# A fused attention and GLU kernel: results stored without the doubled rest, block 0's rest copied at once, stored sums added a step later

## The chip, the cores and the metric

The kernel runs on one core of a Trainium2 chip. The core's engines each work through a queue of their own: TensorE (PE in the profile, with its weight loads as PEld) multiplies matrices, VectorE (DVE) and ScalarE (ACT) do elementwise work, GpSimd (POOL) here does little besides issuing stores, and SyncE (SP) issues loads. An engine takes its instructions strictly in order, so an instruction that waits holds everything behind it on that engine. The metric is the device time of the whole program in microseconds; lower is better.

## The reference

Input `x` has 2048 tokens of 576 features. There are 32 heads of 18, and each token attends to 8 earlier tokens at a distance of 2 (itself included). What is computed, cut to what matters:

```python
def _A_ref(x, wqkv, wo):                      # attention
    qkv = (x @ wqkv).reshape(B, S, 3, 32, 18) ...
    idx = pos[:, None] - (arange(8) * 2)[None, :]
    logits = einsum("bhsd,bhswd->bhsw", q, kg) * scale   # masked where idx < 0
    o = einsum("bhsw,bhswd->bhsd", softmax(logits), vg)
    return o.reshape(B, S, 576) @ wo
def _B_ref(x, w_gate, w_up, w_down):          # GLU, hidden width 4608
    return (sigmoid(x @ w_gate) * (x @ w_up)) @ w_down
h  = x + _A_ref(_layernorm(x), wqkv, wo)
h2 = h + _B_ref(_layernorm(h), w_gate, w_up, w_down)
```

## The kernel before

**Blocks.** The 2048 tokens are cut into four blocks of 512 (even and odd tokens, first and second half), each held as four tiles of 128 tokens. Heads come in four groups `g` of 8 heads (144 columns). An attention unit (b, g) is the attention of one block and one group.

**Precision.** Each fp32 operand of a matmul is split into a rounded part (`th`, `h0h`, ...), written by ACT (L104), and what is left (`tl`, `h0l`, ...), written by DVE (L105); three products of the parts are added in PSUM. Features are 576 = 4 x 128 + 64. The last 64, the *rest*, are kept twice, side by side, to make a fifth chunk of 128: `split_rest` (L107 to L109) rounds both copies on ACT and replaces the second 64 partitions by the remainder on DVE. So a tile that is to be transposed for a matmul has 640 columns (`DX`), the last 64 a copy of columns 512 to 575.

**Attention on DVE.** One unit (`attention`, from L170) multiplies keys by queries (L189, 2 halves), reduces over 18 (L193), takes a softmax, multiplies values by the weights (L215), adds eight terms pairwise (L221, L223, L226). All of it is DVE work, yielded step by step from the generator `att_all`, which the program steps between the matmul groups of the rest. Its units run in the order (0,0), (0,1), (1,0), (0,2), (0,3), (1,1), (1,2), (1,3); those of blocks 2 and 3 come later, under the MLP. Block 0's result goes straight into the tile `tok`; after (0,3), four copies (L428) double its rest. The results of blocks 1 to 3 go by POOL to the scratch `oscr` in DRAM, 144 columns for each unit (L228), and for the last group a second store writes the doubled rest (L230).

**Front of block 0.** `front` transposes `tok` on PE, splits it, multiplies by `wo`, adds to `x`, normalises again, and transposes once more for the MLP. The helper `proj_j` (from L247) is the same chain for one tile of blocks 1 to 3; its `oj` is a tile of 128 tokens loaded back from `oscr`, with 640 columns.

**MLP.** The hidden width is 36 slices of 128. `single` does one slice of two blocks in the ordinary way: products `b` of `th`/`tl` with the weights `w` (L746, L753), a sigmoid on ACT, a product `s<-s,b` on DVE (L766), and its split (`h0h`, `h0l`). `pair` does them by a scheme of seven products in place of eight over matrices cut in two by two; ACT copies some products out (L820, L830, L834), DVE adds others (L825, L839, L844). The products must be taken out of PSUM before PE may reuse a bank. The down projection writes `dp` (L864, L926), which ACT or DVE takes out (L872, L874). Weights come by `load_gu` into `wg` (two buffers, so that a load waits for DVE and ACT to have split the weights two slices earlier), and background loads by `paced`, one behind the other on SP; `oj` is among them. First come 12 `single` slices for blocks 0 and 1 with attention of block 1 and then its projection under them, then 24 `pair` slices, then the same for blocks 2 and 3.

**The end.** Sums of blocks 2 and 3 that were put into DRAM (`h<-ev`) are read back by `load_tails` into `tail` and `more`; after `lag(7)`, seven further steps of the queue, three additions `tail<-tail,more` on DVE (L1240, 128x1152) each take a step, and the last down products are added to `tail` (L874).

**What sets the order.** A scheduler takes the instructions in priority order and writes each engine's queue from its own model of times; `tc.high_priority` raises work, and `tc.issue_after(i)` keeps an instruction from being placed ahead of `i`.

## Time and profile before

| | us |
|---|---|
| median of 3 runs (1580.72 to 1584.34) | 1581.41 |
| the profiled execution | 1584.01 |
| its span | 1582.2 |
| PE busy | 1551.0 (98%) |
| DVE busy | 1255.2 (79%) |
| ACT busy | 879.2 (56%) |
| POOL busy | 199.9 (13%) |
| mean DMA rate | 173 GB/s |

The span is the time from the first instruction to the last of one execution; 1.8 us of the profiled execution lie outside it. Busy shares are averages over stages: DVE is nearly full while attention runs (about 20 to 310 us) and has room later. In the rows below, an instruction stands as engine, line, operation, output<-inputs and shape; `[1.70 <-DVE tok L428]` is idle time ahead of it on its engine, in us, and the instruction that ended it. A row of the waits gives the total, the count and the longest. `L746` is line 746 of the kernel before. Lines of the changed kernel are 1 to 17 higher.

### The profile page before, as it was taken

What the parts mean: (1) busy time and instruction counts of PE and PEld (TensorE: products, weight loads), DVE (VectorE), ACT (ScalarE), POOL (GpSimd) and SP (SyncE); (2) the same over time, 40 slices, a digit from 0 to 9 for tenths busy, and PEclk for the clock granted to TensorE, in tenths of its full rate; (3) what the DMA queues carried; (4) which work ended last, traced back from release to release, by engine and by line L of the source; (5) the groups of instructions that cost most, each with busy time, mean ns of one, the idle gap of its engine ahead of it and who ended that gap; (6) DMA issues with size and microseconds to landing.
All of it is one profiled execution on the core that took longest, in us unless ns stands there. A gap on an engine that the chain in (4) does not pass through costs nothing.

```text
span 1582.2 us, 22347 instructions
## 1 busy us (share of the span) xinstructions
PE 1551.0 (98%) x8520; PEld 1377.3 (87%) x8520; DVE 1255.2 (79%) x1883; ACT 879.2 (56%) x1584; POOL 199.9 (13%) x249
## 2 busy tenths in 40 slices
PE   8999999999999999999999999999999999999998
PEld 7999888887888888888888888888888888888887
DVE  6998999969999999999426588866777776677755
ACT  6632244435555645566542355766777766777660
POOL 2300000020000010000101010112112112111210
PEclk9999999999999999999999999999999999999999
DMA  8646445365566677664683524999899989999983
GB/s 284 215 168 220 179 185 190 108 235 183 133 167 170 164 176 192 157 162 109 161 242 125 181 81 126 193 181 177 170 180 186 173 173 181 173 173 186 181 169 120
DMA packets 77147, 273.95 MB, mean 173 GB/s; under 512 B 8336, under 2 KB 14224, under 8 KB 76144
## 3 DMA queue, kind: packets, MB, share of 16 engines
q0 software_dynamic: 28192, 107.29, 37.5%
q1 hardware_dynamic: 41216, 145.11, 27.2%
q10 hardware_dynamic: 7632, 20.12, 3.3%
q8 instruction: 66, 1.08, 0.3%
q14 instruction: 41, 0.34, 0.1%
HBM read 143.98 MB, written 130.87 MB: 174 GB/s over the span
## 4 chain that ended last, share of the span: by engine, by line
PE 58%; issue 16%; DVE 11%; DMA 8%; POOL 4%; ACT 2%; SPq 0%; ACTq 0%; POOLq 0%; DVEq 0%
PE b L746 27%; PE dp L864 13%; PE dp L926 6%; PE b L753 5%; PE acc L157 4%; POOL h L935 3%; DMA wg<-in_wmlp_dram 3%; DVE pr L189 2%; DVE pr L215 1%; DVE lg L193 1%; DVE w L105 1%; DVE pr L221 1%; PE b L157 1%; PE bgp L157 1%; DMA x<-tok 1%
## 5 line engine op out<-in xcount | busy, mean ns | idle before, releaser
L746 PE MATMUL b<-tl,w 128*128 128x512 f32 x1704 | 432.6, 393 | 5.1 <-ACT s L820 3.2
L746 PEld LDWEIGHTS b<-tl,w 128*128 128x128 f32 x1704 | 307.9, 188 | 63.6 <-ACT s L820 4.7
L746 PE MATMUL b<-th,w 128*128 128x512 f32 x1344 | 346.2, 392 | 1.5 <-DVE s L839 1.5
L746 PEld LDWEIGHTS b<-th,w 128*128 128x128 f32 x1344 | 244.8, 188 | 46.5 <-DVE s L839 1.9
L932 ACT ACTIVATE ev<-dp 128x576 f32<-128x576 f32 x224 | 144.7, 646 | 63.2 <-PE dp L926 58.9
L753 PE MATMUL b<-th,w 128*128 128x512 f32 x568 | 175.7, 390 | 0.0
L104 ACT ACTIVATE w<-wg 128x384 fp32r<-128x384 f32 (+1 forms) x186 | 110.8, 601 | 111.1 <-PE b L753 48.8
L935 POOL DMA_DIRECT2D h<-ev x128 | 110.0, 860 | 458.6 <-ACT ev L932 444.7
L157 PE MATMUL acc<-qw,th 128*128 128x432 f32 x512 | 154.3, 362 | 2.5 <-DVE th L109 2.3
L105 DVE TENSOR_TENSOR w<-wg,w 128x640 fp32r<-128x640 f32 (+1 forms) x186 | 120.8, 656 | 41.3 <-ACT w L104 41.1
L105 DVE TENSOR_TENSOR w<-tw,w 128x512 fp32r<-128x512 f32 x120 | 82.6, 688 | 82.1 <-ACT w L104 81.5
L753 PEld LDWEIGHTS b<-th,w 128*128 128x128 f32 x568 | 106.5, 188 | 23.2
L864 PE MATMUL dp<-d,h1h 128*128 128x288 f32 x640 | 119.9, 297 | 0.0
L864 PE MATMUL dp<-d,h0h 128*128 128x288 f32 x608 | 114.1, 297 | 0.8 <-DVE tail L874 0.8
L872 ACT ACTIVATE stage<-dp 128x576 f32<-128x576 f32 x104 | 66.9, 645 | 70.1 <-PE dp L864 69.8
L157 PEld LDWEIGHTS acc<-qw,th 128*128 128x128 f32 x512 | 96.6, 189 | 8.4 <-DVE th L109 3.5
L864 PEld LDWEIGHTS dp<-d,h1h 128*128 128x128 f32 x640 | 99.7, 190 | 3.0
L104 ACT ACTIVATE w<-tw 128x512 fp32r<-128x512 f32 x120 | 75.4, 628 | 46.5 <-PE b L746 40.0
L864 PEld LDWEIGHTS dp<-d,h0h 128*128 128x128 f32 x608 | 95.1, 190 | 4.3 <-DVE tail L874 1.0
L157 PE MATMUL acc<-qw,tl 128*128 128x432 f32 x256 | 92.6, 362 | 0.1
L189 DVE TENSOR_TENSOR pr<-kw,q 128x2304 f32<-128x2304 f32 x32 | 81.8, 2556 | 8.8 <-DMA kw<-k 8.7
L880 POOL DMA_DIRECT2D h<-stage x26 | 31.0, 1194 | 436.3 <-ACT stage L872 350.1
(310 smaller groups left out, 2955.5 us busy)
## 6 DMA issues: line engine op xcount, KB each, us to landing
h<-ev POOLq DMA_DIRECT2D x96, 576.0 KB, 7.1
wg<-in_wmlp_dram SPq DMA_DIRECT2D x47, 928.0 KB, 5.9
h<-stage POOLq DMA_DIRECT2D x26, 1152.0 KB, 9.5
wg<-in_wmlp_dram SPq DMA_DIRECT2D x36, 640.0 KB, 4.3
kw<-k SPq DMA_DIRECT2D x16, 792.0 KB, 5.2
vw<-v SPq DMA_DIRECT2D x16, 792.0 KB, 4.3
wd<-in_wmlp_dram SPq DMA_DIRECT2D x18, 576.0 KB, 7.4
h<-ev POOLq DMA_DIRECT2D x32, 288.0 KB, 6.9
```

Of the source, the lines that this page charges most:

```text
L104: act.activation(hi, src, AF.Copy)
L105: splits.append(dve.tensor_tensor(lo, src, f32(hi), ALU.subtract))
L157: pe.matmul(ps[:, :n], a[:, c, js], m[:, c], start=k == 0, stop=False)
L189: dve.tensor_tensor(pr, both(kw, u), q[:, us].unsqueeze(2).broadcast_to([P, 2, W, CG]), ALU.mult)
L746: pe.matmul(ps, wt[:, a, k0 + c], xx[:, m + c], start=first and k == 0, stop=k == 5, skip_group_check=True)
L753: pe.matmul(ps, wt[:, a, k0], xx[:, 4], start=False, stop=a == 1, skip_group_check=True)
L864: pe.matmul(ps[:, i, :DH2], a[:, js], d[:, m, i * DH2:(i + 1) * DH2], start=k == 0, stop=k == n)
L872: act.activation(hv, ps, AF.Copy)
L880: pool.dma_start(hacc[b], hs, accum_op=ALU.add, max_dma_last_dim=8 * D)
L926: pe.matmul(ps[:, i, :DH2], a[x][:, js], m[y], start=k in (0, 1, 3) and q == 0, stop=q == 2, skip_group_check=True)
L932: act.activation(hs[:, k % 2], ps[:, :, :DH2], AF.Copy)
L935: pool.dma_start(hsev[:, u, k0:k + 1], hs[:, :k + 1 - k0], accum_op=ALU.add, max_dma_last_dim=8 * D)
```

## The change

Three things are edited.

- **Stores.** `oscr` holds 576 columns, and the store of the doubled rest (L230, three times) is gone. A load of `oj` fetches 576 columns, and `proj_j` makes the copy of the last 64 on ACT (`twin`), once a tile: 12 copies 128x64.
- **Block 0's rest.** Four copies of 128x64 become one of 128x4x64. The first product of unit (1,1) is placed behind that copy and its first reduce behind the last remainder of `split_rest` (`rests[-1]`). The unit (1,1) takes one step and then waits, in program order, until the first two steps of `front` are written (`gate`).
- **Tail.** `lag(7)` becomes `lag(8)`.

```diff
-    oscr = {b: dr.tile([P, NS, DX], F32, name=f"o{b}") for b in (1, 2, 3)}
+    oscr = {b: dr.tile([P, NS, D], F32, name=f"o{b}") for b in (1, 2, 3)}
...
     def split_rest(t, src):
         act.activation(t, src, AF.Copy)
-        dve.tensor_tensor(t[64:128], src[64:128], f32(t[64:128]), ALU.subtract)
+        m = dve.tensor_tensor(t[64:128], src[64:128], f32(t[64:128]), ALU.subtract)
+        rests.append(getattr(m, "ins", m))
...
+            with ExitStack() as way:
+                if (b, g, u) == (1, 1, 0):
+                    way.enter_context(tc.issue_after(ready[0]))
+                dve.tensor_tensor(pr, both(kw, u),
+                                  q[:, us].unsqueeze(2).broadcast_to([P, 2, W, CG]), ALU.mult)
+            yield
+            yield
+            with ExitStack() as way:
+                if (b, g, u) == (1, 1, 0):
+                    way.enter_context(tc.issue_after(rests[-1]))
+                dve.tensor_reduce(lg[:, us].rearrange("p j w h -> p (j w h)"),
...
         if spill:
             pool.dma_start(oscr[b][:, :, g * CG:(g + 1) * CG], o)
-            if g == NG - 1:
-                pool.dma_start(oscr[b][:, :, D:DX], o[:, :, CG - DR:CG])
...
         with tc.high_priority(HI):
+            if twin:
+                act.activation(oj[:, D:DX], oj[:, DM:D], AF.Copy)
             split(th[:, 0:4], tl, pv)
...
-            yield from attention(at, b, g, None if b else o[:, :, g * CG:(g + 1) * CG])
+            unit = attention(at, b, g, None if b else o[:, :, g * CG:(g + 1) * CG])
+            if (b, g) == (1, 1):
+                for _ in range(1):
+                    next(unit)
+                    yield
+                while not gate:
+                    yield
+            yield from unit
             if (b, g) == (0, 3):
-                for j in range(NS):
-                    dve.tensor_copy(o[:, j, D:DX], o[:, j, DM:D])
-                ready.append(b)
+                twin = dve.tensor_copy(o[:, :, D:DX], o[:, :, DM:D])
+                ready.append(getattr(twin, "ins", twin))
...
         for _ in range(2):
             next(fr)
+    gate.append(True)
...
-        paced(t, (xv[e, hf] if i else oscr[b])[:, j])
+        paced(t[:, :D], (xv[e, hf] if i else oscr[b])[:, j])
...
-        yield from lag(7)
+        yield from lag(8)
```

How the order of instructions changes is seen at three places. First, DVE at the end of unit (0,3). `tok` is block 0's result, `pr` and `lg` belong to unit (1,1), and `tl` and `th` are the splits of the transposed `tok`. Before:

```order
L226 TENSOR_TENSOR tok<-kw 128x4x144
L189 TENSOR_TENSOR pr<-kw,q 128x2304
L428 COPY tok<-tok 128x64 x4
L193 TENSOR_REDUCE lg<-pr 128x128
L105 TENSOR_TENSOR tl<-mm,th 128x4x128
L109 TENSOR_TENSOR th<-acc,th 64x128 x3
L109 TENSOR_TENSOR th<-mm,th 64x128
L105 TENSOR_TENSOR tl<-mm,th 128x4x128
```

And now:

```order
L234 TENSOR_TENSOR tok<-kw 128x4x144
L443 COPY tok<-tok 128x4x64
L194 TENSOR_TENSOR pr<-kw,q 128x2304
L106 TENSOR_TENSOR tl<-mm,th 128x4x128
L110 TENSOR_TENSOR th<-mm,th 64x128
L106 TENSOR_TENSOR tl<-mm,th 128x4x128
L110 TENSOR_TENSOR th<-acc,th 64x128 x3
L106 TENSOR_TENSOR tl<-acc,th 128x4x128 x2
L201 TENSOR_REDUCE lg<-pr 128x128
```

The copy has gone ahead of the product, and the reduce behind all the splits.

Second, from the first hidden product `s<-s,b` on DVE to the first transposes of `oj` on PE. On DVE, just ahead of that product, before (`kw<-kw` ends unit (1,1), the `pr` behind it begins (1,2)):

```order
L215 TENSOR_TENSOR pr<-vw,lg 128x2304
L109 TENSOR_TENSOR th<-acc,th 64x128 x2
L221 TENSOR_TENSOR pr<-pr 128x2x576
L109 TENSOR_TENSOR th<-acc,th 64x128
L223 TENSOR_TENSOR kw<-pr 128x2x2x144
L105 TENSOR_TENSOR df<-wg_2024,df 128x576
L105 TENSOR_TENSOR wf<-h,wf 128x640
L105 TENSOR_TENSOR wf<-h,wf 128x256
L226 TENSOR_TENSOR kw<-kw 128x576
L189 TENSOR_TENSOR pr<-kw,q 128x2304
L105 TENSOR_TENSOR wf<-h,wf 128x384
L105 TENSOR_TENSOR df<-h,df 128x576
```

And around it now:

```order
L110 TENSOR_TENSOR th<-acc,th 64x128 x2
L106 TENSOR_TENSOR wf<-h,wf 128x384
L106 TENSOR_TENSOR df<-h,df 128x576
L782 TENSOR_TENSOR s<-s,b_2242 128x512
L229 TENSOR_TENSOR pr<-pr 128x2x576
L106 TENSOR_TENSOR h0l<-s,h0h 128x512
L231 TENSOR_TENSOR kw<-pr 128x2x2x144
L223 TENSOR_TENSOR pr<-vw,lg 128x2304
```

Both halves of the last sums of (1,1) stand behind the first hidden product now. On PE, just ahead of the first transposes of `oj`, before:

```order
L746 MATMUL b_3346<-tl,w_3205 128x512 x6
L746 MATMUL b_3346<-th,w_3205 128x512 x6
L753 MATMUL b_3346<-th,w_3205 128x512 x2
L864 MATMUL dp<-d,h0h 128x288 x2
L864 MATMUL dp<-d,h0l 128x288
L146 MATMUL b_2864<-ident,oj 128x128 x4
```

And now:

```order
L762 MATMUL b_3334<-tl,w_3173 128x512 x6
L762 MATMUL b_3334<-th,w_3172 128x512 x6
L769 MATMUL b_3334<-th,w_3172 128x512 x2
L880 MATMUL dp<-d,h0h 128x288 x2
L880 MATMUL dp<-d,h0l 128x288 x2
L880 MATMUL dp<-d,h0h 128x288 x4
L880 MATMUL dp<-d,h0l 128x288 x2
L880 MATMUL dp<-d,h0h 128x288 x2
L762 MATMUL b_3454<-tl,w_3318 128x512 x2
L148 MATMUL b_2880<-ident,oj 128x128 x4
```

Counted from the first `b` on, 310 products of `b` stand ahead of these transposes in place of 294, and 216 of `dp` in place of 195.

Third, DVE at the end. Before:

```order
L825 TENSOR_TENSOR s<-s,b_14899 128x512
L1240 TENSOR_TENSOR tail_14846<-tail_14846,more_14848 128x1152
L839 TENSOR_TENSOR s<-s,b_14898 128x512
L1240 TENSOR_TENSOR tail_14851<-tail_14851,more_14853 128x1152
L844 TENSOR_TENSOR s<-s,b_14900 128x512
L1240 TENSOR_TENSOR tail_14851<-tail_14851,more_14856 128x1152
L766 TENSOR_TENSOR s<-s,b_14898 128x512
L766 TENSOR_TENSOR s<-s 128x512
L874 TENSOR_TENSOR tail_14846<-tail_14846,dp 128x2x288 x3
```

And now:

```order
L841 TENSOR_TENSOR s<-s,b_14905 128x512
L855 TENSOR_TENSOR s<-s,b_14904 128x512
L1257 TENSOR_TENSOR tail_14852<-tail_14852,more_14854 128x1152
L860 TENSOR_TENSOR s<-s,b_14906 128x512
L1257 TENSOR_TENSOR tail_14857<-tail_14857,more_14859 128x1152
L782 TENSOR_TENSOR s<-s,b_14904 128x512
L782 TENSOR_TENSOR s<-s 128x512
L1257 TENSOR_TENSOR tail_14857<-tail_14857,more_14862 128x1152
L890 TENSOR_TENSOR tail_14852<-tail_14852,dp 128x2x288 x3
```

Each addition has moved one product back, the third behind both `s` of L782.

On ACT, near 391 us of the profile, the copy `s<-b` of L820 (now L836) that stood behind three splits and a step L845 of the slice ahead now stands ahead of the split `w<-wg 128x640`. On SP, `vw` of unit (1,2) has two more weight loads ahead of it, and `kw` and `vw` of (1,3) one more.

14 lines of the change are left out of this document (7 added, 7 removed).

## The prediction

> **What bounds the kernel now.** I read the page first, then the waits of TensorE (PE), then the instructions around each wait.
>
> ```profile
> PE 1551.0 (98%) x8520; PEld 1377.3 (87%) x8520; DVE 1255.2 (79%) x1883; ACT 879.2 (56%) x1584; POOL 199.9 (13%) x249
> ```
>
> PE works for 1551.0 of the span's 1582.2 us. A change that leaves the matmuls as they are can at most win back the rest, and much of that is the start. So the waits of PE are the table to read (total us, how often, longest):
>
> ```profile
> PE b L146 <- DMA oj<-o: 4.2, 1, 4.2
> PE b L746 <- ACT s L820: 3.2, 3, 2.4
> PE acc L157 <- DVE th L109: 2.3, 2, 1.6
> PE mm L150 <- DVE tok L428: 1.7, 1, 1.7
> PE b L746 <- DVE s L839: 1.5, 1, 1.5
> ```
>
> Together 12.9 us, in four places. VectorE (DVE) is the engine behind two of them; how full it is there is seen in two stretches, block 0's front and the stretch from the first hidden product to the end of attention (columns: length; busy us of PE, PEld, DVE, ACT, POOL; clock, DMA share, GB/s):
>
> ```profile
> 185.30:227.20 41.90, 41.40 (x246) 37.95 (x247) 39.44 (x74) 15.91 (x38) 3.22 (x5) 1.00 0.41 152
> 227.20:308.50 81.30, 80.19 (x431) 69.84 (x430) 77.86 (x94) 36.05 (x61) 0.71 (x1) 1.00 0.42 152
> ```
>
> In the second stretch DVE idles 3.44 us of 81.30 and PE 1.11: the two are nearly level, so DVE work that comes into it lengthens it.
>
> **1. The copy and splits of block 0's rest.** DVE and PE in order of time (start, us):
>
> ```profile
> 178.10 0.76 DVE L226 TENSOR_TENSOR tok<-kw 128x576 f32<-128x576 f32 x1
> 178.78 2.55 DVE L189 TENSOR_TENSOR pr<-kw,q 128x2304 f32<-128x2304 f32 x1
> 181.25 0.49 DVE L428 COPY tok<-tok 128x64 f32<-128x64 f32 x4
> 181.65 2.55 DVE L193 TENSOR_REDUCE lg<-pr 128x128 f32<-128x2304 f32 x1
> 184.23 0.69 DVE L105 TENSOR_TENSOR tl<-mm,th 128x512 fp32r<-128x512 f32 x1
> 184.95 0.71 DVE L109 TENSOR_TENSOR th<-acc,th 64x128 fp32r<-64x128 f32 x3
> 181.79 0.33 PE L150 MATMUL mm<-ident,tok 128*128 128x128 f32 x1 [1.70 <-DVE tok L428]
> 185.30 0.46 PE L157 MATMUL acc<-qw,th 128*128 128x432 f32 x1 [1.65 <-DVE th L109]
> ```
>
> PE waits 1.70 for a copy that stands behind the product L189, then 1.65 for a split behind the reduce L193. In the new order the copy follows the sum at 178.86. One copy of 128x4x64 costs between one small copy (the four overlap and end 0.49 after the first starts, some 0.12 each) and all four; I take 0.3. It ends at about 179.2, before PE wants it at 180.1, so the 1.70 goes. The product then runs to 181.7. Behind it stand `tl<-mm`, `th<-mm`, `tl<-mm` (0.65, 0.27, 0.65) and the first `th<-acc` (0.3), which ends near 183.6; PE restarts at 183.6 in place of 185.30. Of 3.35 us of waits 1.7 are won, bounds 1.2 and 2.1 (the product is still ahead of the splits, so the second wait shrinks only by what the first gave). The reduce is now late for unit (1,1), whose end no engine but DVE awaits.
>
> **2. What that pushes behind the first hidden product.** The unit (1,1) now stops for the front steps. By the two orders, seven DVE instructions that stood ahead of the first `s<-s,b` now stand behind it: two L221, two L223, one L215, one L226, one L189.
>
> ```profile
> 227.15 0.69 DVE L766 TENSOR_TENSOR s<-s,b 128x512 f32<-128x512 f32 x1 [1.25 <-PE b L753]
> L215 DVE TENSOR_TENSOR pr<-vw,lg 128x2304 f32<-128x2304 f32 x32 | 81.8, 2557 | 0.6
> L221 DVE TENSOR_TENSOR pr<-pr 128x1152 f32<-128x1152 f32 x32 | 43.4, 1356 | 0.4
> L223 DVE TENSOR_TENSOR kw<-pr 128x576 f32<-128x576 f32 x32 | 24.2, 757 | 0.5
> ```
>
> That is 2x1.36 + 2x0.76 + 2.56 + 0.76 + 2.55 = 10.1 us, and three more MLP splits of 0.6 come in between: 11.9 us more in the stretch that was level. The front is PE's (busy 41.40 of 41.90), so the DVE time freed there is idle.
>
> **3. The end of attention and the loads of oj.** How block 1's last sum reaches PE now:
>
> ```profile
> 307.78 0.75 DVE L226 TENSOR_TENSOR kw<-kw 128x576 f32<-128x576 f32 x1
> 309.46 6.85 DMA o<-kw
> o<-kw POOLq DMA_DIRECT2D x1, 288.0 KB, 4.5
> o<-kw POOLq DMA_DIRECT2D x1, 128.0 KB, 6.9
> 319.42 0.90 PE L146 MATMUL b<-ident,oj 128*128 128x128 f32 x3 [4.23 <-DMA oj<-o]
> o<-kw POOLq DMA_DIRECT2D x1, 288.0 KB, 8.4
> ```
>
> The second line is from the chain of waits: the 128 KB store of the doubled rest, issued second, lands at 316.31 and SyncE (SP) loads oj behind it. The 288 KB store, issued near 308.8, takes 4.5 and is down at 313.3. Without the rest store the loads start 3.0 earlier: sum to oj becomes 319.42 - 307.78 - 3.0 = 8.6 us. The last line is the same kind of store in the window from 185 to 240, where it took 8.4; with that nothing is saved, so this part is worth 0 to 3.0, and I take 3.0, since that store met loads at over 400 GB/s and the window here is empty. By the Trainium skill ("DMA: Bandwidth & Descriptors", Anatomy of one DMA) a GpSimd-issued DMA takes about 2.0 us and its bytes at 436 GB/s, an estimate of 2.3 us for 128 KB; by that the rest store would be down before the main one and its removal would give nothing, for a sum of 0.1 instead of -2.9. The trace has 6.9 us for it, so the trace decides.
>
> The last sum now starts at 225.45 (first product, 1.7 earlier) + 80.63 + 11.9, less the idle that a full DVE takes back, 2.2 of 3.44: at 315.8. oj is there at 324.4. PE meanwhile has more to do. In the new order 16 matmuls of `b` and 21 of `dp` more stand ahead of the first transposes of oj:
>
> ```profile
> 299.80 1.81 PE b L746 x8
> 1555.03 22.67 PE dp L864 x168
> ```
>
> 16 x 0.226 + 21 x 0.135 = 6.4 us, so the kernel before would begin the same transposes at 319.42 + 6.4 = 325.8. The net gain when oj is reached is 1.4 us, between 2.7 (all idle taken back) and a loss of 0.6 (none, main store 1 us late). The front's 1.7 is in this and not counted again. PE still waits some 4.5 us there. Behind it there is 6.4 us less work to cover the projection of block 1; PE already waits 0.2 to 0.4 there twice, so a loss of 0 to 3; I take 0.3.
>
> **4. Twelve copies on ScalarE (ACT) in place of doubled loads.** The nearest row is a copy of the same shape:
>
> ```profile
> L142 ACT ACTIVATE tok<-tok 128x64 f32<-128x64 f32 x8 | 2.1, 263 | 0.0
> ```
>
> 12 x 0.26 = 3.2 us on an engine with 44% free, hidden by PE's products; if they were not, 3.2 would be the loss. But each waits for its load on ACT's queue with other splits behind it, which the load's landing can hold by 1 to 1.7 us in block 3. I take a loss of 0.2, bounds 0 and 1.5. The loads lose 32 of 160 KB each; nothing in the trace waits for those bytes alone.
>
> **5. The wait on a weight load at 391.** From the chain, ACT and PE:
>
> ```profile
> 381.67 8.78 DMA wg<-in_wmlp_dram
> 390.53 0.74 ACT L104 ACTIVATE w<-wg 128x640 fp32r<-128x640 f32 x1 [4.38 <-DMA wg<-in_wmlp_dram]
> 393.31 1.88 PE L746 MATMUL b<-tl,w 128*128 128x512 f32 x7 [2.37 <-ACT s L820]
> ```
>
> The copy L820, which frees PE's bank, stands behind four ACT instructions, the first of which waits for this load. In the new order this copy stands ahead of that split, so PE need not wait for the load. But the load itself may be up to 2.7 later against PE, and the split weights are wanted soon after. From -2.4 to +0.5; I take -1.7.
>
> **6. The stored sums a step later.** DVE and PE near the end:
>
> ```profile
> 1546.95 1.36 DVE L1240 TENSOR_TENSOR tail<-tail,more 128x1152 f32<-128x1152 f32 x1 [5.02 <-DMA tail<-h]
> 1548.22 0.68 DVE L839 TENSOR_TENSOR s<-s,b 128x512 f32<-128x512 f32 x1
> 1549.88 1.36 DVE L1240 TENSOR_TENSOR tail<-tail,more 128x1152 f32<-128x1152 f32 x1 [0.98 <-DMA tail<-h]
> 1551.16 0.68 DVE L844 TENSOR_TENSOR s<-s,b 128x512 f32<-128x512 f32 x1
> 1551.76 1.35 DVE L1240 TENSOR_TENSOR tail<-tail,more 128x1152 f32<-128x1152 f32 x1
> 1553.03 0.68 DVE L766 TENSOR_TENSOR s<-s,b 128x512 f32<-128x512 f32 x1
> 1555.03 0.53 PE L864 MATMUL dp<-d,h0h 128*128 128x288 f32 x2 [0.78 <-DVE tail L874]
> ```
>
> L839 stands behind an addition that waits for a load; PE loses 1.49 there. Now L839 goes first and that gap closes. But the additions don't move with it: the first still starts at 1546.95, L844 finds its product at 1551.07 - 1.49 = 1549.6, the second addition runs from 1550.2, the two L766 to 1552.8, the third addition, now ahead of the `tail<-tail,dp` sums that free PE's bank, to 1554.1, and the first of these ends near 1554.8. PE goes on at 1554.8 instead of 1555.03. Of the 1.49 some 0.3 is kept, bounds 1.5 (if the loads come earlier by what was won before) and a loss of 0.5 (if the third addition's place costs a whole 1.36 at a bank).
>
> **Sum.** -1.4 + 0.3 + 0.2 - 1.7 - 0.3 = -2.9 us. The profiled execution took 1584.01 us (span 1582.2 and 1.8 around it), 2.6 above the median of the runs; from it 1581.1, and against the median, 1581.41, which the result is compared with, 1578.5.
>
> **Rivals.**
>
> *All the waits go* (faster). If the second front wait goes too (1.65), oj arrives as PE reaches it (4.2) and 391 is clean (2.4), the sum is 8 us: 1573.4. For it: each is a wait on something that the change moves. Against: the 10.1 us of DVE work in a stretch with 3.44 of idle.
>
> *A load of unit (1,3) comes late* (slower). On SP's queue, two more weight loads now stand ahead of the load `vw` of (1,2) and one more ahead of `kw` and `vw` of (1,3), among them loads that wait for DVE and ACT to free their buffers. If DVE then finds its operand missing, the nearest row is a wait of the same unit type:
>
> ```profile
> DVE pr L189 <- DMA kw<-k: 8.7, 2, 4.8
> ```
>
> With 4.8 of that and none of the idle taken back (2.2), the last sum starts at 322.8, oj comes at 331.4, 5.6 later than in the kernel before, and with the other terms (-1.5) the sum is +4.1: 1585.5. It decides against the change from a last sum later than 321.9. For it: DVE and PE level over 81 us; against: those two waits are both in the first 130 us, and none in this stretch.
>
> *The main store is as late as the rest store was* (same). With 8.4 for the 288 KB the 3.0 of part 3 is lost: +0.1, about 1581.5.
>
> **Chances.** A measurement of this kernel tells a change from none from about 0.2%, 3.2 us: faster is under 1578.2, slower over 1584.6. The case forecast has 0.50 with its own range of 1576 to 1581, 0.23 of it faster and 0.27 same. All waits gone 0.22, faster. The late load, or another way in which DVE's fuller stretch holds PE, 0.20, slower. The late store 0.08, same, with 0.02 of it slower. That makes 0.45 faster, 0.33 same, 0.22 slower. The range goes from 1572.5 (all waits and the tail's whole 1.5) to 1585.5 (the late load).
>
> **What would show it.** PE restarts near 183.6 with no wait on the copy. The first hidden product is near 225.4. The last `kw<-kw` before the oj loads starts at 314 to 318, the store behind it takes about 4.5, and PE's wait for oj is 3 to 7. No wait of PE on L820's successor at about 391. At the end the wait on L839 is gone and that on the tail sums has grown from 0.8 to about 2. I would be wrong by a last sum past 322, a store of 8 us, new PE waits between 320 and 395, or if DVE idles less in the front than the 10 us I move.

## The result, and the profile after

The changed kernel is slower, by about 20 us. Its median is 1601.82 us (1597.89 to 1603.09), against 1582.41 us for the kernel before in the same comparison: a ratio of 1.0124, with a 95% interval of 1.0106 to 1.0141. The forecast was 1578.5 with a range to 1585.5. The profiled execution took 1601.56 us and its span is 1599.8 us, 17.6 more than the span before.

The first line of the page of the changed kernel answers to the one that opens the prediction:

```profile
PE 1558.1 (97%) x8520; PEld 1381.7 (86%) x8520; DVE 1255.9 (79%) x1880; ACT 882.7 (55%) x1596; POOL 201.0 (13%) x246
```

PE does the same 8520 matmuls, but is busy 7.1 us longer. So some 7 of the 17.6 us are matmuls that ran at a lower granted clock (shown below), and the other 10.5 are waits. The waits of PE in the changed kernel (total us, how often, longest):

```profile
PE b L762 <- ACT w L105: 4.0, 1, 4.0
PE b L762 <- ACT s L836: 3.4, 2, 2.9
PE dp L880 <- DVE stage L890: 3.4, 2, 3.0
PE acc L159 <- DVE th L110: 3.3, 2, 2.7
PE dp L880 <- ACT stage L888: 2.7, 2, 1.7
...
PE b L762 <- DVE w L106: 2.2, 1, 2.2
...
PE dp L880 <- DVE tail L890: 1.9, 1, 1.9
PE mm L148 <- DVE tok L234: 1.7, 1, 1.7
```

The wait of 4.2 for `oj` is gone (0.47 is left of it), and so is that on L839. In their place stand waits that the kernel before did not have, or had smaller. The places of the four longest behind block 0's front are seen on PE's timeline (start, us of work; the wait in brackets):

```profile
296.41 0.53 PE L880 MATMUL dp<-d,h0h 128*128 128x288 f32 x2 [3.05 <-DVE stage L890]
...
307.85 1.80 PE L762 MATMUL b<-tl,w 128*128 128x512 f32 x4 [2.18 <-DVE w L106]
...
391.36 0.79 PE L762 MATMUL b<-tl,w 128*128 128x512 f32 x1 [3.96 <-ACT w L105]
...
443.42 0.98 PE L762 MATMUL b<-tl,w 128*128 128x512 f32 x3 [2.93 <-ACT s L836]
```

Laid side by side by matmul work done (each matmul counted with the time that its kind usually takes), the changed kernel is 0.3 us behind at 280 us of the kernel before, 9.9 behind at 310, 2.8 at 350 (it no longer waits for `oj`), 12.5 at 390, 9.6 at 400 (the kernel before has its own wait there), 15.8 at 440, 15.5 at 800, 17.5 at 820 and 17.6 at the end. Nearly all of the loss is made between 280 and 440 us, and most of it behind 350; 2 us come at 820, in block 3's projection.

Why PE waits at 293 is read on DVE (timeline of the changed kernel):

```profile
228.93 0.69 DVE L782 TENSOR_TENSOR s<-s,b 128x512 f32<-128x512 f32 x1 [4.53 <-PE b L769]
...
286.36 2.54 DVE L201 TENSOR_REDUCE lg<-pr 128x128 f32<-128x2304 f32 x1
288.82 0.74 DVE L890 TENSOR_TENSOR stage<-stage,dp 128x576 f32<-128x576 f32 x1
289.48 2.55 DVE L194 TENSOR_TENSOR pr<-kw,q 128x2304 f32<-128x2304 f32 x1
291.95 0.68 DVE L782 TENSOR_TENSOR s<-s,b 128x512 f32<-128x512 f32 x1
292.55 2.54 DVE L201 TENSOR_REDUCE lg<-pr 128x128 f32<-128x2304 f32 x1
295.01 0.68 DVE L106 TENSOR_TENSOR h0l<-s,h0h 128x512 fp32r<-128x512 f32 x1
295.61 0.74 DVE L890 TENSOR_TENSOR stage<-stage,dp 128x576 f32<-128x576 f32 x1
...
322.68 0.75 DVE L234 TENSOR_TENSOR kw<-kw 128x576 f32<-128x576 f32 x1
```

Three attention instructions of 2.5 us stand within 9 us, and the sum L890, which frees the bank that PE wants for `dp`, stands behind the third. The last sum of block 1 starts at 322.68, where 315.8 had been forecast. In the stretch from the first hidden product to the end of that sum DVE is busy 89.97 of 94.45 us (columns as in the prediction):

```profile
228.98:323.43 94.45, 88.80 (x454) 76.73 (x453) 89.97 (x105) 40.17 (x66) 1.48 (x2) 0.96 0.38 141
```

Before, it was 77.86 of 81.30. So 12.1 us of DVE work came in, where 11.9 had been counted; but the idle time of DVE did not shrink, it grew from 3.44 to 4.48, and PE, which had idled 1.11 us in this stretch, idled 5.65.

And the clock. These rows are one-microsecond windows behind the wait that ends at 391.36 (the figure third from the end is the granted clock):

```profile
391.00:392.00 1.00, 0.64 (x1) 0.28 (x1) 0.14 (x1) 1.00 (x3) 0.00 (x0) 0.50 1.07 439
...
395.00:396.00 1.00, 1.00 (x3) 0.76 (x3) 0.74 (x1) 0.56 (x1) 0.00 (x0) 0.50 1.15 396
396.00:397.00 1.00, 1.00 (x4) 0.77 (x3) 1.00 (x1) 0.00 (x0) 0.00 (x0) 0.53 0.87 267
397.00:398.00 1.00, 1.00 (x6) 0.83 (x5) 1.00 (x2) 0.00 (x0) 0.00 (x0) 1.00 0.96 393
```

For over five microseconds behind the wait of 3.96 the clock is at half, which costs a further 2.4 us of the time in which PE works there. Over the whole run such stretches behind pauses of PE cost about 11 us in the changed kernel and 4.3 before. No term of the prediction held such a cost.

### The profile page after: what moved, and what is told of

It is laid out like the page before. It is cut to its first block, busy times and chain, and to the rows that moved or that the text cites. A ratio compares the mean times of both kernels' runs of the same rounds, so it can differ in the third digit from the quotient of the medians.

```text
span 1599.8 us, 22352 instructions
## 1 busy us (share of the span) xinstructions
PE 1558.1 (97%) x8520; PEld 1381.7 (86%) x8520; DVE 1255.9 (79%) x1880; ACT 882.7 (55%) x1596; POOL 201.0 (13%) x246
## 4 chain that ended last, share of the span: by engine, by line
PE 62%; issue 14%; DVE 9%; DMA 8%; POOL 4%; ACT 2%; SPq 0%; ACTq 0%; POOLq 0%; DVEq 0%
PE b L762 30%; PE dp L880 13%; PE dp L942 6%; PE b L769 6%; PE acc L159 4%; POOL h L951 3%; DMA wg<-in_wmlp_dram 3%; DVE pr L194 2%; DMA oj<-o 1%; DVE lg L201 1%; PE b L159 1%; PE bgp L159 1%; DVE pr L223 1%; DMA kw<-k 1%; DVE w L106 1%
## 5 line engine op out<-in xcount | busy, mean ns | idle before, releaser
L762 PE MATMUL b<-tl,w 128*128 128x512 f32 x1704 | 437.3, 396 | 12.1 <-ACT w L105 4.0
```

The lines of the kernel that those rows point to most:

```text
L762: pe.matmul(ps, wt[:, a, k0 + c], xx[:, m + c], start=first and k == 0, stop=k == 5, skip_group_check=True)
```

## The experiments

Three theories were tested, alone or together. *The copies:* the 12 copies on ScalarE wait for their loads in ACT's queue and hold what stands behind them. *The full stretch:* the attention work that the gate puts behind the first hidden product fills DVE, and every small piece of MLP work comes late. *The weight load:* something makes the load that PE waits for at 387 us slow; first the loads of the next attention units were suspected, then stores on GpSimd's queue. Medians are given with the ratio to the kernel before of the same comparison and its 95% interval.

### One part undone, one part alone

**Without the gate.** From the changed kernel:

```diff
-            if (b, g) == (1, 1):
-                for _ in range(1):
-                    next(unit)
-                    yield
-                while not gate:
-                    yield
             yield from unit
```

> The changed kernel with only the wait of unit (1,1) for the front taken out (the copy at once, the product behind it, the first reduce behind the splits, the stores and the later sums stay). Theory G, the gate: it pushed seven DVE instructions (10.1 us) behind the first hidden product, made DVE the bound from 290 to 310, the last sum late, and through SP's queue the weight loads at 387 and 430 late; without it 1576 to 1583, first hidden product at about 226, last sum at 308 to 310, no PE wait over 3 us between 380 and 445. Theory S, the stores: the twelve ACT copies and the other order that the smaller loads give make the pair phase late; then this stays at 1595 or over.

Measured: 1590.11 us, 1.0054 (1.0035 to 1.0072). 11.7 of the 20 us go with the gate. The rest stays, so the gate is not alone: by matmul work done this kernel is level with the kernel before from 390 to 780 us, then loses 4.6 us by 820 and 3.7 at the end, in a wait for the tail sums. At the front the other edits do worse without it: PE waits longer here, once, than in the kernel before twice (1.70 and 1.65).

```profile
187.52 0.46 PE L159 MATMUL acc<-qw,th 128*128 128x432 f32 x1 [4.25 <-DVE th L110]
```

**With the old stores.** The changed kernel with the store of the doubled rest and the loads of 640 columns put back, without the 12 copies:

```diff
+            if g == NG - 1:
+                pool.dma_start(oscr[b][:, :, D:DX], o[:, :, CG - DR:CG])
...
-            if twin:
-                act.activation(oj[:, D:DX], oj[:, DM:D], AF.Copy)
...
-        paced(t[:, :D], (xv[e, hf] if i else oscr[b])[:, j])
+        paced(t, (xv[e, hf] if i else oscr[b])[:, j])
```

> The changed kernel with the doubled rest stored and loaded as before, so no copies on ACT; the gate, the copy at once, the order of the splits and the later sums stay. Theory G: stays slow, 1600 to 1606, since the rest store comes back on top (0 to 3 us more at the loads of oj). Theory S: back to 1580 to 1585.

Measured: 1594.75 us, 1.0085 (1.0062 to 1.0108). So the new stores cost some 6 to 7 us on top of the gate.

**The stores alone.** The kernel before with only the edits of stores, loads and copies.

```diff
-            if g == NG - 1:
-                pool.dma_start(oscr[b][:, :, D:DX], o[:, :, CG - DR:CG])
...
+            if twin:
+                act.activation(oj[:, D:DX], oj[:, DM:D], AF.Copy)
...
-        paced(t, (xv[e, hf] if i else oscr[b])[:, j])
+        paced(t[:, :D], (xv[e, hf] if i else oscr[b])[:, j])
```

> The kernel before with the stores, loads and ACT copies of the change alone. Theory G: faster than before by the rest store, 0 to 4 us, or 1577 to 1583; PE's wait for oj falls from 4.2 to about 1.2 and its clock there stays at 1.00. Theory S: 1595 or over.

Measured: 1587.49 us, 1.0033 (1.0017 to 1.005): slower, where the prediction's terms for these edits (3.0 won, 0.2 lost) give a gain. Most of the loss appears in block 3's projection. ACT and PE there (timeline):

```profile
801.36 1.54 PE L753 MATMUL b<-tl,w 128*128 128x512 f32 x6
802.43 0.26 ACT L254 ACTIVATE oj<-oj 128x64 f32<-128x64 f32 x1 [1.12 <-DMA oj<-o]
806.37 0.26 ACT L254 ACTIVATE oj<-oj 128x64 f32<-128x64 f32 x1 [3.69 <-DMA oj<-o]
806.54 1.17 ACT L879 ACTIVATE stage<-dp 128x576 f32<-128x576 f32 x2
...
807.22 0.54 PE L871 MATMUL dp<-d,h1h 128*128 128x288 f32 x2 [2.50 <-ACT stage L879]
...
809.40 2.63 PE L753 MATMUL b<-tl,w 128*128 128x512 f32 x6
```

A copy of 0.26 us waits 3.69 us for its load. The two copies out of PSUM behind it wait as well, PE waits 2.50 for the first, and then runs at half clock: six matmuls take 2.63 us where six of the same kind took 1.54 ahead of it. By matmul work done this kernel is 2.9 us ahead of the kernel before at 780 us, and 1.5 behind at 820.

**The later additions alone.** The kernel before with

```diff
-        yield from lag(7)
+        yield from lag(8)
```

> The kernel before with the stored sums one step later, nothing else: only DVE's order at the end differs. Both theories: within 1.5 us of the kernel before; the wait of 1.49 on L839 is gone and the wait for the tail sums grows from 0.8 to 1.6 to 2.2. A gain or loss of over 2 us would speak against my working of the end.

Measured: 1581.07 us, 0.9999 (0.9984 to 1.0014). No difference that can be told. The wait of 1.49 on L839 is gone; near the end only this one remains:

```profile
1548.64 0.53 PE L873 MATMUL dp<-d,h0h 128*128 128x288 f32 x2 [0.29 <-DVE tail L883]
```

### The copies on ScalarE

**On GpSimd instead.** The kernel of the stores alone with

```diff
-                act.activation(oj[:, D:DX], oj[:, DM:D], AF.Copy)
+                pool.tensor_copy(oj[:, D:DX], oj[:, DM:D])
```

> The stores of the change alone, with the twelve copies of the rest on GpSimd in place of ScalarE; DVE's and SP's orders stay those of that part alone. Theory H, the held queue: in the stores-alone kernel ACT's copy waited 3.69 us for its load at 802 to 806, the copy-out of dp stood behind it, PE waited 2.5 and then ran its products at 0.44 us in place of 0.23 for some 5 us, so about 5 us in all; with the copies off ACT that wait is gone and the time is 1579 to 1583, a gain of 4 to 8 against the stores alone. Rival: the loss came from the other order of the pair phase or from the loads; then it stays at 1586 to 1589.

Measured: 1582.72 us, 1.0009 (0.9995 to 1.0023), against 1.0033 with the copies on ACT. Its PE shows no wait between 795 and 815 us. The held queue is shown as the cause of most of the loss of the stores alone.

**The rest loaded twice.** The kernel before without the store of the doubled rest and without any copy; the last 64 columns are loaded a second time.

```diff
-        paced(t, (xv[e, hf] if i else oscr[b])[:, j])
+        paced(t[:, :D], (xv[e, hf] if i else oscr[b])[:, j])
+        if not i:
+            paced(t[:, D:], oscr[b][:, j, DM:D])
```

> The kernel before without the rest store; the doubled 64 columns of oj come by a second small load from the same place, so there is no copy on any engine. Twelve more loads on SP of 256 bytes a row. Theory H: no wait on ACT's stage at 805, 1577 to 1583. Rival (the loads cost as much as the store did): 1584 to 1588, with a PE wait for oj of 4 or more.

Measured: 1584.07 us, 1.0024 (1.001 to 1.0039). The wait for `oj` shrinks from 4.23 to 1.74 here too, but the wait on the weights near 387 grows:

```profile
387.42 0.80 PE L751 MATMUL b<-tl,w 128*128 128x512 f32 x1 [4.14 <-ACT w L105]
```

What is won at `oj` is lost 70 us later here. In the stores alone and without the gate the same wait is 2.35 and 2.11, much as in the kernel before (2.37); there the gain lasts to about 780 us and goes in block 3's projection. So in none of these kernels is the time shorter for the removal of the rest store.

### How full DVE is

**The first reduce not held.** The changed kernel, whose reduce may go ahead of the last remainder of `split_rest`:

```diff
-                if (b, g, u) == (1, 1, 0):
-                    way.enter_context(tc.issue_after(rests[-1]))
```

> The changed kernel without the rule that puts the first reduce of (1,1) behind the splits; the gate stays. By its order the same seven DVE instructions (10.1 us) stand behind the first hidden product as in the changed kernel, and 42 products of b and 45 of dp more than before stand ahead of oj (16 and 21 in the changed kernel). Theory G (the gate's shift of DVE work and of PE's cover): stays slow, 1594 to 1606. Rival: the reduce behind the splits is what costs; then 1586 to 1590, the time without the gate.

Measured: 1592.23 us, 1.0078 (1.0057 to 1.0098). The waits at 293 and 305 are gone, and at 350 us this kernel is ahead of the kernel before; then it waits at another place, at 363 us for a split on ACT:

```profile
367.08 0.79 PE L760 MATMUL b<-tl,w 128*128 128x512 f32 x1 [4.35 <-ACT tl L105]
```

**Five steps before the gate.** Unit (1,1) takes five steps ahead of the front, so that less of it lies behind the first hidden product:

```diff
-                for _ in range(1):
+                for _ in range(5):
```

> The changed kernel with five steps of (1,1) ahead of the gate in place of one. By its order 5.4 us of DVE work in place of 10.1 stand behind the first hidden product, but PE has the same 15 products of b and 26 of dp more ahead of oj. If the DVE work moved is what costs (DVE had 3.4 us of idle to take it), the stretch from 290 to 310 has PE waits of 2 in place of 6 and the time falls to 1590 to 1596; if the cover taken from the work behind oj costs, the weight-load waits at 387 and 440 stay and the time is 1598 to 1604.

Measured: 1588.06 us, 1.0052 (1.0033 to 1.0072), 13.8 less than the changed kernel. The last sum of block 1 starts at 314.67 instead of 322.68, and there is no wait over 0.5 us between 270 and 380.

**Less attention work in the stretch.** The changed kernel, in which the second half of the logits of (1,2) and (1,3) is copied from the first, so that their products and reduces are left out (the busy time of DVE falls by 9.7 us):

```diff
+            if (b, g) in ((1, 2), (1, 3)) and u:
+                for _ in range(3):
+                    yield
+                dve.tensor_copy(lg[:, us], lg[:, 0:2])
+                continue
```

> The changed kernel with the second half of the logits of units (1,2) and (1,3) copied from the first half (a product and a reduce less in each, some 10 us of DVE work; those logits are left out). Theory D: DVE's fuller stretch up to the last sum is what made everything behind it late. Then the last sum is at 308 to 313, no PE wait of 2 or more between 290 and 310, the waits at 387 and 440 shrink to 0 to 2.5, and the time is at most 4 us above that of the lighter kernel before: 1580 to 1586, or 15 to 20 under the full changed kernel. Rival: the order that follows (weight loads, pair slices) is late by itself: 1592 to 1600.

Measured: 1585.1 us, 1.0021 (1.0004 to 1.0038): 16.7 us less than the changed kernel. PE still waits 3.01 near 385, more than was expected, but for a copy on ACT and with no low clock behind it; near 443 it waits 1.44.

**The same in the kernel before.** The same five lines.

> The kernel before with the same logits of (1,2) and (1,3) left out, as the reference for the lighter changed kernel. DVE had 3.4 us of idle in 81 there, and PE's wait for oj of 4.2 is behind it: 1574 to 1582, 0 to 7 us under the full one.

Measured: 1581.04 us, 0.9988 (0.9972 to 1.0004). Here the same relief is worth nothing that can be told. Without these 8 to 10 us of DVE work the two kernels stand 4 us apart, with them 20. The pair does not change the DVE work alone: in the lighter changed kernel six stores of zeros on GpSimd's queue go out at 342.52 us, in the changed kernel at 378.10, and that place was worth some 5.5 us in the changed kernel (see the weight load near 387, below). By that estimate the DVE work and its order have some 10 of the 16 us. The stretch from 228 to 308 us in the changed kernel, and in the lighter one:

```profile
228.00:308.00 80.00, 74.35 (x397) 65.00 (x396) 75.89 (x86) 34.40 (x56) 1.48 (x2) 0.98 0.39 148
```

```profile
228.00:308.00 80.00, 80.00 (x432) 70.12 (x431) 77.17 (x98) 37.79 (x63) 2.19 (x3) 1.00 0.43 153
```

In the lighter one PE is busy all 80 us and at full clock, although DVE is busy longer; it has 98 instructions done there instead of 86. In the changed kernel DVE and PE wait for each other by turns: DVE idles 4.1 us of the 80 and PE 5.65. So a full DVE alone does not cost this. The traces point to long attention instructions close together, with short ones behind them that PE wants; no kernel here changes their order alone.

### The combination

**The changed kernel with the copies on GpSimd.**

```diff
-                act.activation(oj[:, D:DX], oj[:, DM:D], AF.Copy)
+                pool.tensor_copy(oj[:, D:DX], oj[:, DM:D])
```

> The changed kernel with only the twelve copies moved from ScalarE to GpSimd; the orders of PE, DVE and SP stay row for row. Theory H (the held queue) with the gate's part separate from it: the wait for stage at 823 and what follows it go, 1594 to 1598 against 1601.8. Rival (in the full change the copies cost nothing of their own): 1600 to 1604.

Measured: 1598.52 us, 1.01 (1.0065 to 1.0134). About 3 us less, with an interval that still overlaps that of the changed kernel.

**Five steps, and the copies on GpSimd.** Both edits shown above.

> Five steps ahead of the gate and the copies on GpSimd. Theory H: the PE wait of 3.3 at 806 and 1.7 of clock after it go, so 1581 to 1584 in place of 1588. It would then end level with the kernel before, though 6 us ahead of it at 340 us of PE's work: the waits at 384 take that back.

Measured: 1582.37 us, 1.0007 (0.999 to 1.0024). This is the time of the kernel before. By matmul work done it is 6 us ahead of it at 340 us and 0.5 behind at 390: it loses all in one wait, the same as in the changed kernel.

```profile
388.59 1.22 PE L762 MATMUL b<-tl,w 128*128 128x512 f32 x2 [5.17 <-ACT w L105]
```

**The free reduce, and the copies on GpSimd.**

> The gate without the rule on the reduce, and the copies on GpSimd; orders of PE, DVE and SP as in the run with that rule out. Theory H: the wait of 3.95 at 805 and 1.7 of clock go: 1585 to 1588 in place of 1592.

Measured: 1589.37 us, 1.0048 (1.0029 to 1.0067).

**Pauses put into the kernel before.** To price the clock by itself, DVE got needless additions ahead of L825 at five slices of the pairs:

```diff
+            for _ in range({52: 8, 55: 10, 58: 12, 61: 14, 64: 17}.get(c, 0)):
+                dve.tensor_tensor(s2, s1, b2, ALU.add)
```

> The kernel before with 8, 10, 12, 14 and 17 needless additions of 128x512 on DVE ahead of the sum L825 in five pair slices of the second half, which hold the product banks; nothing is left out. It makes PE pauses of some 0 to 6 us in a calm stretch, to see what a pause costs beyond itself. Theory C (the clock): after a pause of over 3 us the granted clock falls to 0.5 for 3.4 us or twice that, so 1.7 to 3.4 us are lost on top; after a pause of under 2 us mostly nothing. The time rises by the sum of the pauses and 3 to 9 us more. Rival: a pause costs only itself, and the low clock in the other traces belongs to the places, not to the pauses.

Measured: 1598.41 us, 1.0104 (1.0068 to 1.014). It did not tell what it was made for. In place of five pauses of rising length PE made clusters of short ones, the longest 1.92 us. Behind two of them, which begin at 1242.94 and 1248.69 us, came one stretch at half clock, 1.7 us lost; behind one of 1.47 us came none.

### The weight load near 387

**Small loads of the next units.** Behind the slow load of `wg` stand, on SP's queue, `q`, `kw` and `vw` of the next attention units. In this kernel, made from the changed one, they load 16 of 128 partitions for (2,0) and (2,1), and the rest is set to zero on GpSimd:

```diff
+            few = 16 if (b, g) in ((2, 0), (2, 1)) else P
+            if few < P:
+                for z in (q, kw, vw):
+                    pool.memset(z.rearrange("p j c -> p (j c)"), 0.0)
-            sp.dma_start(q.rearrange("p j c -> p (j c)"), qscr[b][g])
+            sp.dma_start(q.rearrange("p j c -> p (j c)")[:few], qscr[b][g][:few])
...
```

> The changed kernel; the loads of q, kw and vw of the units (2,0) and (2,1) fetch 16 of 128 partitions (the rest of the tiles is zeroed on GpSimd, so block 2's attention in two groups is not computed from its data). Up to PE's wait at 387 the orders of PE and DVE are those of the changed kernel. Theory L, the load: the weights for the wait at 387 were issued at 379.6 and took 10.9 us because four attention loads (2.7 MB) were issued in the 5 us behind them; with an eighth of those bytes they land by 386 to 387, PE's wait of 3.96 falls under 1 and the low clock behind it goes: 6 us less by 400 us. Theory D, the late DVE: the split work and the freeing of the buffers are what comes late; then PE's wait stays over 2.5.

Measured: 1599.08 us, 1.0101 (1.0084 to 1.0118), and the wait stays:

```profile
387.27 0.79 PE L766 MATMUL b<-tl,w 128*128 128x512 f32 x1 [4.05 <-ACT w L105]
```

These loads are not its cause. What is left is the other engine that issues transfers. In the kernel before (timeline of POOL):

```profile
348.95 4.28 POOL L1055 DMA_DIRECT2D h<-z  x6 [0.30 <-POOL z L1052]
378.51 1.24 POOL L880 DMA_DIRECT2D h<-stage  x1 [25.28 <-DVE stage L874]
```

And in the changed kernel (timeline of POOL, SP, ACT):

```profile
376.19 1.26 POOL L896 DMA_DIRECT2D h<-stage  x1 [16.27 <-DVE stage L890]
378.10 4.28 POOL L1072 DMA_DIRECT2D h<-z  x6 [0.30 <-POOL z L1069]
379.62 0.33 SPq L718 DMA_DIRECT2D wg<-in_wmlp_dram  x1
...
390.57 0.74 ACT L105 ACTIVATE w<-wg 128x640 fp32r<-128x640 f32 x1 [6.05 <-DMA wg<-in_wmlp_dram]
```

Six stores of zeros, 288 KB each, set the parts of `h` into which sums are later added. Before, they went out at 349. In the changed kernel a store of 1152 KB (`h<-stage`), which waits for a DVE sum until 376.19, stands ahead of them on POOL's queue. That store is not late itself (378.51 before); the two have changed places in the order that the scheduler wrote. This is so in every kernel here with the gate, but for the lighter one and those in which the zeros are moved early, and in none without the gate. So the zeros, 1.7 MB, go out 1.5 us ahead of the weight load, which then lands after 10.9 us. The ten microseconds at the load's issue, first in the kernel before:

```profile
378.00:388.00 10.00, 10.00 (x46) 8.29 (x45) 10.00 (x13) 3.34 (x6) 1.24 (x1) 1.00 1.03 269
```

and in the changed kernel:

```profile
376.00:386.00 10.00, 9.91 (x43) 7.66 (x43) 9.52 (x14) 5.16 (x9) 5.88 (x8) 1.00 0.84 168
```

The DMA engines are nearly as busy (0.84 against 1.03), but move 168 GB/s instead of 269.

**The zeros early.** The changed kernel; a small tile of zeros from the start, and the six stores behind the store of unit (1,1). The order on the other four queues is the same to the last row:

```diff
+    z = cst.tile([P, ZN], F32, name="z")
+    pool.memset(z, 0.0)
...
+            if (b, g) == (1, 1):
+                with tc.issue_after(spills[-1]):
+                    for k in range(6):
+                        pool.dma_start(hsev[:, k // 3, 1 + 2 * (k % 3)]...,
+                                       z.unsqueeze(1).broadcast_to([P, 2 * DH2 // ZN, ZN]))
...
-            z = at2.tile([P, DH2], F32, name="z")
-            pool.memset(z, 0.0)
-            for u in range(2):
-                for k in (1, 3, 5):
-                    pool.dma_start(hsev[:, u, k], z.unsqueeze(1).broadcast_to([P, 2, DH2]))
```

> The changed kernel with one thing moved: the six zero stores of 288 KB that stand on GpSimd's queue behind the stores of tail stage (issued near 378 us in its profile) are issued behind the store of unit (1,1), near 255 us, from a tile of 48 columns. The orders of the other four queues stay as they are. If these stores delay the weight load issued at 379.6 (10.9 us in the changed kernel), that load takes under 8.5 us, PE's wait near 387 (3.96) shrinks below 1.5 with the granted clock kept, and the median is 1595 to 1598.5. If the DVE's fuller stretch alone makes the loss, the wait stays over 3 and the median is within 0.15% of the changed kernel's 1601.8, so 1599.4 to 1604.

Measured: 1596.3 us, 1.0089 (1.007 to 1.0108). The zeros go out at 240.51, and the load takes 7.5 us instead of 10.9:

```profile
377.62 0.33 SPq L728 DMA_DIRECT2D wg<-in_wmlp_dram  x1
385.15 0.74 ACT L109 ACTIVATE w<-wg 128x640 fp32r<-128x640 f32 x1 [2.61 <-DMA wg<-in_wmlp_dram]
...
385.94 0.50 PE L772 MATMUL b<-tl,w 128*128 128x512 f32 x1 [0.52 <-ACT w L109]
387.46 1.66 PE L772 MATMUL b<-tl,w 128*128 128x512 f32 x6 [1.02 <-ACT s L856]
```

The wait of 3.96 has become 0.52 and 1.02, and the clock stays full behind it. The place of the zero stores is shown as the cause of that wait. It is not the only way to such a wait: where the rest was loaded twice, the zeros went out at 347.69, and PE waited 4.14 there.

The wait near 440 is another matter: with early zeros it is still 2.92 us. In the changed kernel it goes back to the next weight load. SP issues this load at 421.17 us, where the kernel before issued it from 405.64 on: the load of `q` of a later unit stands ahead of it on SP's queue and waits for a product on DVE until 412.75, and then the load itself waits for DVE to split the weights before it. It lands 10.1 us after its issue. ACT has waited 5.87 us for it by then, and the copy L836, which PE needs, stands behind ACT's splits of these weights. With five steps ahead of the gate PE waits only 0.2 us there. What makes this load late was not tested by itself.

**Five steps, copies on GpSimd, zeros early.**

> The kernel with five steps of unit (1,1) ahead of the gate and the 12 copies on GpSimd (1582.4), with the zero stores moved early in the same way. If the zero stores cost what their place on the weight load suggests, 1577 to 1580 and so faster than the kernel before (its wait near 387 is then under 1.5); if not, 1581 to 1584.

Measured: 1574.91 us (1571.63 to 1576.45), 0.9955 (0.9939 to 0.9971). This version beats both kernels, the one before by 6 us. Its page has PE busy 1547.6 us, 3.4 less than in the profile before at the same 8520 matmuls, and among its waits behind the first 100 us are these, the largest first (waits of PE; that of 3.1 is in block 0's front, at 184 us):

```profile
PE acc L163 <- DVE th L114: 3.7, 2, 3.1
PE b L152 <- DVE tl L110: 2.5, 1, 2.5
PE dp L890 <- DVE tail L900: 2.0, 1, 2.0
...
PE b L772 <- ACT w L109: 0.7, 1, 0.7
...
PE b L152 <- DMA oj<-o: 0.5, 1, 0.5
```

Whether early zeros would also help the kernel before by themselves was not tried; its zeros already go out 30 us ahead of that load.

**The free reduce, copies on GpSimd, zeros early.**

> The kernel with the free first reduce and the copies on GpSimd (1589.4), with the zero stores moved early in the same way. If the zero stores take part in the loss, 1584 to 1587; if not, 1588 to 1591. Together with the other two this says whether the effect of the zero stores is the same in three orders of DVE.

Measured: 1586.88 us, 1.0034 (1.0021 to 1.0047). That is 2.5 us below the same kernel with late zeros, at the edge of what was expected, with overlapping intervals. The large pause of this order, 4.74 us from 368.86 on, is one for a split of block 1's operands on ACT, not for the weights; it stayed. So the zeros matter where PE stands on the weight load, and what makes the pause of this order is left open.

## Why the prediction was wrong, point by point

**1, the front: about right.** PE restarted at 185.68 against the forecast 183.6. But the last sum of `tok` began at 179.97 here and at 178.10 in the profile before; from that sum to the restart it took 5.71 us in place of 7.20, so 1.5 were won, of 1.7 forecast. The wait on the copy is gone, as was forecast; what PE waits for now (1.75) is the sum itself. The profile before shows an early front: its first hidden product is at 227.15, and in the kernel with the later additions alone, whose order is the same there, at 230.02. Against that one the changed kernel (228.93) wins 1.1; one profile each doesn't tell more.

**2 and 3, DVE's fuller stretch: the step that failed.** The amount of work was right (12.1 us for 11.9), what it does was not. The prediction said that the stretch from the first hidden product grows by 11.9 less 2.2 of idle, and put the cost of this at the arrival of `oj` and behind it only: a net gain of 1.4 when `oj` is reached, then "a loss of 0 to 3; I take 0.3". The stretch grew by 13.1 us, none of the idle came back, it began 3.5 us later than forecast, and the last sum came 6.9 later. And PE did not wait for `oj` at the end of it, it waited inside it, at 293 and 305, for a DVE sum and a DVE split that came late. At 350 us PE was 2.8 us behind, where these terms had it 1.1 ahead; the rest of the 15.5 us lost between 280 and 440 came at the weights, at 387 (below) and at 440. That it hangs on the order of DVE's work is shown by the five steps ahead of the gate, which give back 13.8 of the 20 us with the zeros still late (373.30 us); the pair of lighter kernels, 4 us apart, points the same way. The rival of a late load had the right sign and, with a last sum past 321.9, the right mark, but not the mechanism: no load of unit (1,3) was waited for. Its other half, "another way in which DVE's fuller stretch holds PE", was the case; the rival had a chance of 0.20 and a price of 1585.5, 16 us too low. The bound of 0.6 on the loss at `oj` was also too small by the prediction's own figures: 1.4 less the 2.2 of idle is a loss of 0.8, and 1.8 with the store 1 us late.

**3, the rest store: the price was about right, the gain did not last.** The wait for `oj` fell by 2.5 to 2.9 us in the three kernels that took the store out of the order before, near the 3.0 of the text. Where the rest was loaded twice, PE then reached the weights of 387 that much earlier than they could come; in the stores alone the gain lasted to 780 us and went with the held copies. The prediction called the window of the main store empty; a weight load of 928 KB was issued at 309.27 in it, and the DMA engines moved 427 GB/s in the microsecond from 312. The main store's 4.5 us was measured beside that load, so the price does not hang on this.

**4, the copies on ACT: right in kind, mis-sized.** "I take a loss of 0.2, bounds 0 and 1.5." Moving the copies to GpSimd gave back 4.8 us in the stores alone (1587.49 to 1582.72), 5.7 with five steps, about 3 in the other two orders. One copy waited 3.69 us, PE 2.50 behind it, and the clock took another 1.7. The loads are 320 KB each before the change, not 160, of which 32 go; no term hangs on that.

**5, the wait on the weights: wrong.** The copy L836 did go ahead of the split, so PE no longer waited for the copy; it waited for the split weights themselves, 3.96 us in place of 2.37, and behind it the clock fell. From 350 to 400 us PE lost 6.8, where 1.7 were to be won. The prediction followed the order on ACT and on SP. It did not read GpSimd's queue, where, with the gate, six stores had changed places with a store that waits for DVE. Moving those six back was worth about 5.5 us in the changed kernel and 7.5 in the one with five steps.

**6, the tail: right.** PE no longer waits for L839 and waits longer for the tail sums: 1.93 us in the changed kernel in place of 1.49 and 0.78, a gain of 0.3 as forecast. Alone the edit has a ratio of 0.9999.

**The sum.** The low end of the range, 1572.5, should have been 1571.9 by its own words (1573.4 less 1.5); the measured time lies far beyond the other end. The steps from the changed kernel to the best version are 13.8 us (five steps ahead of the gate, DVE's order), 5.7 (copies) and 7.5 (zeros), 26.9 together: the loss and the 6 us below the kernel before. The same steps taken singly from the changed kernel give 13.8, 3.3 and 5.5, so they don't quite add up: 22.6 singly, 26.9 in order. The size of each is a difference of medians with some 3 us of spread; their order in time and the waits named are read from the traces.

## What to carry to other kernels

When work moves into a stretch in which two engines are level, count the short instructions that the other engine waits for and ask behind how many long ones each will stand; an idle share of some per cent is no reserve. Read the order on every queue, those included that only issue stores: a store that waits for an engine holds the transfers behind it and sends them into a time when something else needs the memory. A small copy that waits for a load belongs on an engine on whose queue nothing urgent stands behind it.

## What the runs showed of the hardware

The granted clock of PE falls after pauses much shorter than I had thought worth pricing. In the 20 traces there are, behind the first 100 us and up to PE's last matmul, 132 pauses of PE of more than 1.2 us and 67 stretches at a clock of 0.5. Of the 33 pauses of at least 3 us, 30 were followed within 5 us by such a stretch; of 49 between 2 and 3 us, 32; of 50 shorter ones, 11, some of these close ahead of or behind another pause. 47 of the stretches are 3.41 us long, and 42 cost about 1.7 us each; the other 20 are twice as long and cost 2.0 to 3.1, as part of them falls into the pause. So a pause of 3 us and more costs on average 2 us more than its length, and such losses (about 11 us against 4.3) account for nearly all of the 7.1 us by which PE's busy time grew. The Trainium skill ("TensorE: Matmul & The Clock Gate", Part 1: The HAM clock gate) has the array at half rate after at least one idle window of about 3.4 us, and says that such a window runs freely; the length of 3.4 us agrees with the 3.41 of these stretches, but here pauses of 2 to 3 us were enough two times in three.

The same weight load of 928 KB took 7.5 us with the zero stores early, and 10.9 with six stores of 288 KB issued 1.5 us ahead of it.
